# Places for round two's split weights taken after their words have landed, the order written with dearer table changes, and one subtraction moved to GpSimd

## Chip, cores and metric

One core of a Trainium2 chip runs the whole program. The metric is the device time of one execution in microseconds (us); lower is better. Engines: PE is TensorE, ACT is ScalarE, DVE is VectorE, POOL is GpSimd, SP is SyncE, which here issues DMAs only.

## Reference

Attention that keeps the 32 largest scores of each row, then two MLPs, all in fp32. Cut to what matters:

```python
# q, k, v: (2, 8, 576, 64)
scores = q @ k.T / sqrt(64)
kth    = 32nd largest score of each row
attn   = softmax(where(scores >= kth, scores, -1e9))
x = (attn @ v) as 1152 tokens x 512
h = x @ w_in;  x = (h * tanh(softplus(h))) @ w_out      # 512 -> 2048 -> 512, Mish
h = x @ w2_in; out = (relu(h) ** 2) @ w2_out            # 512 -> 2048 -> 512
```

The MLP weights come as float64 words and have to be made fp32 on the chip.

## The kernel before

The 1152 tokens go in four **rounds** of 256, 320, 320 and 256 tokens. A round is the attention of its tokens (four pairs of heads, each of 4 or 5 *tiles* of 128 rows by 576 scores; 72 tiles in all) and then its two MLPs: in-phase, out-phase, in-phase, out-phase, each over 8 of the 32 weight pieces of 512 KB. Attention of later rounds stands beside the MLPs of earlier ones. (The code counts rounds from 0; "round two" of the change is `r == 1`, here always called round 1.)

A tile: scores on PE (L466, tile `ps`), copied by ACT to `s`; the 32 largest found on DVE by four MAX8 and three MATCH_REPLACE8 (L480, L483, L484); two small POOL operations make `nm` (L495, L496); ACT makes the mask with Prelu and then Exp (both write `e`, L498 to L500); PE transposes `e`, ACT copies the result to `pt`, and PE multiplies by v (L563).

Weights: `convert` reads the float64 words of a piece (1024 KB), makes fp32 with two ACT operations (`cu` with Prelu, `raw` or `stage`) and one on DVE (L693), and writes them to DRAM as `kept` (512 KB). Round 0 multiplies with the fp32 words `w` themselves. Round 1 splits each piece into hi and lo parts (tile `wt`, three places): `fetch` loads `w` from `kept` (three places, tag `cf`), ACT copies hi (L744), POOL subtracts lo in four parts (L262), the matmuls of L781 use both, and `keep` writes both to DRAM (`both`, 1024 KB). Rounds 2 and 3 load hi and lo from `both`. From round 1 on the activations are split too: `xh`, `xl` and `gh`, `gl`; `gl` is a subtraction of 128x320 or 128x256 (`sub`, L255), on the engine that the letter of `GL` names for the round: "v" is DVE, "g" POOL.

ACT holds one table of functions at a time. Mish is in another table than Exp; the program holds an ACT_TABLE_LOAD wherever the next operation needs the other one, and one stands ahead of a Prelu that follows Mish too.

**What sets the order.** All engines run their instructions in the order in which they are written, and `Order` (L40 to L153) writes them: it plays the program with an assumed duration for every operation, and at each moment an engine takes the ready operation with the lowest rank. A generator yields `(engine, duration, rank, function[, table])`, a semaphore for a place, an event, or a number (a delay). An operation that names a table other than the current one has 4.0 added to its rank. Tile semaphores make the real waits; the played times decide the order alone.

```python
yield act(0.78, 8, e, s, AF.Prelu, bias=nm[:, 0:1], scale=UP, alpha=2.0 ** 120)   # names no table
yield act(0.85, 8, e, e, AF.Exp, "exp", ...)
yield act(1.07, 12, both[:, 0], w)                       # hi of round 1, rank 12
yield from wide(6, ALU.subtract, both[:, 1], w, ...)     # lo, four parts on POOL
```

Of the kernel before, what the change touches and what calls it, by code (L numbers as in the profile page):

```python
# [9 lines left out]
F32 = mybir.dt.float32  # L10
# [11 lines left out]
BUFS = {"s": 4, "e": 2, "r": 3, "w": 2, "kt": 2, "vt": 3, "qt": 2, "kT": 4, "cu": 4, "cf": 3, "wt": 3, "h": 3, "x1": 2, "pt": 1}  # L22
CONV_EVERY = 6.0
EARLY = 11
GL = "gvggg"
PARTS = 4


class Sem:
# [13 lines left out]
class Order:  # L43
# [69 lines left out]
    def issue(self, e):  # L113
        if self.free[e] > self.now or not self.ready[e]:
            return

        def rank(entry):
            x = entry[3]
            return ((x[2]() if callable(x[2]) else x[2]) + (4.0 if len(x) > 4 and x[4] != self.table else 0.0), entry[1])

        entry = min(self.ready[e], key=rank)
        self.ready[e].remove(entry)
        _, _, gen, x = entry
        value = self.written(x[3])
        t = x[1]
        if len(x) > 4 and x[4] != self.table:
            self.table = x[4]
            t += self.SWITCH
        self.free[e] = self.now + t
        self.last[gen] = e  # L130
        self.at(self.free[e], 0, lambda: self.step(gen, value))
        self.at(self.free[e], 1, lambda: self.issue(e))
# [32 lines left out]
def topk_attention_two_mlps(  # L165
# [50 lines left out]
    def give(*names):  # L216
        for t in names:
            sim.give(sems[t])
# [225 lines left out]
    def tile_of(p, j, a, rank, unit, pair):  # L444
# [50 lines left out]
            nc.gpsimd.tensor_scalar(out=nm[:, 0:1], in0=thr, scalar1=-UP, scalar2=None, op0=ALU.mult)  # L495
            nc.gpsimd.tensor_scalar(out=nm[:, 1:2], in0=thr, scalar1=mx[:, 0, 0:1], scalar2=scale, op0=ALU.subtract, op1=ALU.mult)  # L496

        yield ("POOL", 0.4, 1, biases)  # L498

        yield act(0.78, 8, e, s, AF.Prelu, bias=nm[:, 0:1], scale=UP, alpha=2.0 ** 120)  # L500
        give("s")
        yield act(0.85, 8, e, e, AF.Exp, "exp", bias=nm[:, 1:2], scale=scale / UP, accum_out=acc[:, a:a + 1])
        sim.set(unit[1][a])
# [27 lines left out]
    def unit_end(j, unit, pair):  # L531

        acc, _, done = unit[:3]
        yield sems["r"]
        r_ = new([P, 2, D], F32, "r")
        z = acc if j < 2 else acc[:, 0:1]
        yield ("POOL", 0.2, 1, lambda: nc.gpsimd.tensor_scalar(out=z, in0=z, scalar1=1e-9, scalar2=None, op0=ALU.add))
        yield ("DVE", 0.16, 3, lambda: nc.vector.reciprocal(z, z))
        if j < 2:
            sums = acc[:, 0:2].rearrange("p (a o) -> p a o", o=1).to_broadcast([P, 2, D])  # L540
            yield ("POOL", 0.4, 1, lambda: nc.gpsimd.tensor_tensor(out=r_, in0=sums, in1=one2, op=ALU.mult))
        else:
            yield act(0.3, 10, r_, same, scale=z)
        pair["r"][j] = r_.rearrange("p a d -> p (a d)")
        sim.set(unit[5])

    def pair_end(p, units, pair):
# [44 lines left out]

        yield act(evict_time(n), 9, inv[:, 0:n], pp[:, 0:n])
        give("ps_t")
        yield ("DVE", 0.6, 4, scaled)
        give("ps_x")
        x1_left[r] -= 1
# [71 lines left out]
    def convert(i):  # L669

        src, a, m = pieces[i]
        n = NW
        kind, at = raw_places.pop(0)
        if kind == "stage":
            both = stage[:, at * 2 * n:(at + 1) * 2 * n]
        else:
            both = new([P, 2 * n], F32R, "wt", "raw")
        raw = both.bitcast(I32).rearrange("p (m t) -> p m t", t=2)  # L680
        yield from sim.dma(lambda: nc.sync.dma_start(out=raw.rearrange("p (a m) t -> p a (m t)", a=a), in_=src), 1024, 20)
        yield sems["cu"]
        w = new([P, n], F32, "cu")
        lo, hi = raw[:, :, 0], raw[:, :, 1]
        R = 20 + 0.01 * i

        yield act(1.16, R, w, hi.bitcast(F32), AF.Prelu, scale=2.0 ** -112, alpha=-2.0 ** 32)

        yield act(1.16, R, lo, lo.bitcast(U32), bias=-0.499, scale=LOW3)
        wi = w.bitcast(I32)
        yield ("DVE", 1.65, lambda: 15 if x1_done[0].done or i < EARLY else 25, lambda: nc.vector.scalar_tensor_tensor(out=wi, in0=wi, scalar=3, in1=lo, op0=ALU.logical_shift_left, op1=ALU.bitwise_or))  # L693
        raw_places.append((kind, at))
        sim.give(raw_sem)
        kept[i] = dr.tile([P, n], F32, tag=f"k{i}", name=f"kept{i}")
        yield from sim.dma(lambda: nc.sync.dma_start(out=kept[i], in_=w), 512, 15)
        give("cu")
        sim.set(kept_done[i])
        if i == NP - 1:  # L700

            for d in kept_done:
                yield d
            for _ in range(BUFS["wt"]):
                sim.give(wt_sem)
            sim.set(stage_free)
# [6 lines left out]
            yield CONV_EVERY  # L713

    got = [Ev() for _ in range(NR * NP)]
    ready = {}

    def fetches():
        for i in range(NR * NP):
            r, j = divmod(i, NP)  # L720
            yield kept_done[j]
            yield (sems["cf"] if r == 0 else wt_sem)
            if r == 1:
                yield sems["cf"]
            if r > 1:
                yield both_done[j]
            sim.spawn(fetch(i, r, j))
            yield 0.3

    def fetch(i, r, j):  # L730

        if r < 2:
            w = new([P, NW], F32, "cf", "w")
            yield from sim.dma(lambda: nc.sync.dma_start(out=w, in_=kept[j]), 512, 12)
            ready[i] = [w]
        if r:
            both = new([P, 2, NW], F32R, "wt", "wt")
            ready[i] = [both[:, 0], both[:, 1]]
            if r == 1:
                yield act(1.07, 12, both[:, 0], w)  # L740
                yield from wide(6, ALU.subtract, both[:, 1], w, both[:, 0].bitcast(F32))
                give("cf")
                sim.spawn(keep(j, both, i))
# [265 lines left out]
```

## Time and profile before

| | us |
|---|---|
| median of 3 runs (lowest, highest) | 778.89 (775.28, 780.21) |
| the profiled execution | 773.01 |
| its span, first to last instruction | 771.2 |
| PE busy in the span | 649.1 |
| ACT, DVE, POOL busy | 513.1, 470.1, 249.2 |
| mean granted clock of PE | 0.931 of full speed |

Between the profiled execution and its span lie 1.8 us, taken as fixed. The span has five stretches by what the MLPs do: attention of round 0 alone (to 139 us), Mish of round 0 (to 197), the rest of round 0 (to 331), round 1 (to 551), rounds 2 and 3 (to the end). Round 1 divides at 415, 457 and 512 us into in, out, in and out-phase. A busy PE is counted from modelled ends of pipelined matmuls.

### The profile page before, as it was taken

The numbers are of one execution on the slowest core, as the hardware profiler recorded it, in microseconds if no ns is written. First come the engines' busy times: TensorE is split into PE (matmuls) and PEld (weight loads), VectorE is DVE, ScalarE is ACT, GpSimd is POOL, SyncE is SP. The second block draws the span as 40 slices with busy tenths as digits, with TensorE's granted clock in tenths as the row PEclk, the third lists the DMA queues.
The fourth block names the chain that finished last, engine by engine and source line by source line (L and its number), as shares of the span: only waits on it lengthen the run. The fifth ranks groups of instructions, "written<-read, shape, count | busy, mean of one in ns | idle before, by whom it ended". The sixth has DMA issues, their size and how long they took to land.

```text
span 771.2 us, 11656 instructions
## 1 busy us (share of the span) xinstructions
PE 649.1 (84%) x4056; PEld 569.3 (74%) x4056; DVE 470.1 (61%) x889; ACT 513.1 (67%) x917; POOL 249.2 (32%) x453
## 2 busy tenths in 40 slices
PE   5463565878997979976878998798999999999997
PEld 2342344666876767865777898687899999999997
DVE  3797999787887895998999999995100000100000
ACT  4797865699887976689999779875351272251540
POOL 2233122111221120445535667556341041040330
PEclk9975665999999989998889999899999999999999
DMA  7999920765799976675765688369988888899995
GB/s 199 285 338 329 348 58 18 264 247 164 260 306 364 311 251 199 192 229 167 255 192 207 229 293 301 141 250 338 340 309 295 289 311 292 299 338 366 343 358 196
DMA packets 95290, 201.83 MB, mean 262 GB/s; under 512 B 36352, under 2 KB 61440, under 8 KB 82944
## 3 DMA queue, kind: packets, MB, share of 16 engines
q1 hardware_dynamic: 94144, 200.83, 76.0%
q8 instruction: 32, 0.52, 0.3%
q10 hardware_dynamic: 1088, 0.26, 0.2%
q14 instruction: 26, 0.21, 0.1%
HBM read 146.01 MB, written 52.69 MB: 258 GB/s over the span
## 4 chain that ended last, share of the span: by engine, by line
PE 41%; DMA 22%; ACT 14%; DVE 11%; POOL 5%; SPq 4%; issue 2%; ACTq 0%; POOLq 0%; DVEq 0%
PE pm L781 33%; DMA w<-kept 8%; DMA wt<-both 5%; DVE w L483 4%; POOL wt L262 4%; DVE mx L484 4%; ACT e L249 3%; ACT L249 3%; PE ps L466 3%; SPq L311 2%; PE px L563 2%; ACT wt L249 2%; DMA kt<-in_k 1%; PE pt L509 1%; DMA raw<-in_moe_w_in 1%
## 5 line engine op out<-in xcount | busy, mean ns | idle before, releaser
L781 PE MATMUL pm<-xh,wt 128*128 128x320 f32 (+1 forms) x768 | 170.1, 308 | 2.9 <-DMA wt<-both 1.7
L484 DVE MAX8 mx<-w 128x8 f32<-128x576 f32 x216 | 164.4, 761 | 7.4
L781 PE MATMUL pm<-gh,wt 128*128 128x320 f32 (+1 forms) x768 | 166.0, 302 | 3.3 <-DMA wt<-both 1.2
L781 PEld LDWEIGHTS pm<-xh,wt 128*128 128x128 f32 x768 | 130.4, 194 | 4.3 <-ACT h L249 3.1
L781 PEld LDWEIGHTS pm<-gh,wt 128*128 128x128 f32 x768 | 126.7, 188 | 4.5 <-DMA wt<-both 2.2
L781 PE MATMUL pm<-xl,wt 128*128 128x320 f32 (+1 forms) x384 | 117.5, 306 | 0.2
L781 PE MATMUL pm<-gl,wt 128*128 128x320 f32 (+1 forms) x384 | 115.1, 300 | 0.0
L483 DVE MATCH_REPLACE8 w<-mx,w 128x576 f32<-128x576 f32 x144 | 106.9, 742 | 0.0
L262 POOL TENSOR_TENSOR wt<-w,wt 128x256 fp32r<-128x256 f32 x128 | 91.6, 742 | 35.9 <-ACT wt L249 30.2
L255 POOL TENSOR_TENSOR gl<-h,gh 128x320 fp32r<-128x320 f32 (+1 forms) x64 | 51.6, 806 | 147.7 <-ACT gh L249 111.3
L509 PE MATMUL pt<-ident,e 128*128 128x128 f32 x288 | 50.7, 305 | 43.0 <-ACT e L249 23.6
L509 PEld LDWEIGHTS pt<-ident,e 128*128 128x128 f32 x288 | 37.5, 154 | 53.2 <-ACT e L249 27.4
L249 ACT ACTIVATE h<-pm 128x320 f32<-128x320 f32 (+1 forms) x112 | 45.2, 413 | 45.8 <-PE pm L781 41.8
L781 PEld LDWEIGHTS pm<-xl,wt 128*128 128x128 f32 x384 | 74.4, 194 | 0.6 <-DVE xl L255 0.6
L781 PEld LDWEIGHTS pm<-gl,wt 128*128 128x128 f32 x384 | 72.3, 188 | 0.1
L962 DVE COPY ot<-pm 128x256 f32<-128x256 f32 x16 | 6.7, 421 | 105.1 <-PE pm L954 52.8
L249 ACT ACTIVATE pt<-pt 128x640 f32<-128x640 f32 x72 | 50.4, 700 | 28.3 <-PE pt L511 27.9
L255 DVE TENSOR_TENSOR xl<-pm,xh 128x320 fp32r<-128x320 f32 (+1 forms) x12 | 5.6, 463 | 101.0 <-ACT xh L249 101.0
L495 POOL TENSOR_SCALAR nm<-mx 128x1 f32<-128x1 f32 x72 | 25.1, 349 | 127.9 <-DVE mx L484 127.6
L781 PE MATMUL pm<-gh,w 128*128 128x256 f32 x256 | 62.2, 393 | 4.2 <-DMA w<-kept 4.2
L249 ACT ACTIVATE e<-s,nm 128x576 f32<-128x576 f32 x72 | 55.6, 772 | 14.5 <-POOL nm L495 14.0
L249 ACT ACTIVATE e<-e,nm 128x576 f32<-128x576 f32 x72 | 55.8, 776 | 6.4 <-POOL nm L496 0.5
(94 smaller groups left out, 1171.8 us busy)
## 6 DMA issues: line engine op xcount, KB each, us to landing
wt<-both SPq DMA_DIRECT2D x64, 1024.0 KB, 5.2
w<-kept SPq DMA_DIRECT2D x64, 512.0 KB, 5.9
both<-wt SPq DMA_DIRECT2D x32, 1024.0 KB, 4.9
kept<-cu SPq DMA_DIRECT2D x32, 512.0 KB, 7.0
raw<-in_moe_w_in SPq DMA_DIRECT2D x9, 1024.0 KB, 8.9
raw<-in_moe_w_out SPq DMA_DIRECT2D x9, 1024.0 KB, 8.3
stage<-in_moe_w_in SPq DMA_DIRECT2D x7, 1024.0 KB, 6.5
stage<-in_moe_w_out SPq DMA_DIRECT2D x7, 1024.0 KB, 9.4
```

Of the source, the lines that this page charges most:

```text
L249: op = ("ACT", t, rank, lambda: nc.scalar.activation(out, in_, func, **kw))
L255: return ({"g": "POOL", "v": "DVE"}[e], t, rank, lambda: eng.tensor_tensor(out=out, in0=in0, in1=in1, op=ALU.subtract))
L262: yield ("POOL", 0.05 + 0.0024 * n, rank, lambda: nc.gpsimd.tensor_tensor(out=out[:, z], in0=in0[:, z], in1=in1[:, z], op=op))
L311: f = lambda o=o, x=x, e=eng if i >= 3 else nc.sync: e.dma_start(out=o, in_=x)
L466: nc.tensor.matmul(sp[:, i, 0:HK], q_, k_[:, i * HK:(i + 1) * HK], start=l == 0, stop=l == len(steps) - 1)
L483: nc.vector.match_replace(out=w, in_to_replace=mx[:, i - 1, :], in_values=s if i == 1 else w, imm_value=LOWEST)
L484: nc.vector.max(out=mx[:, i, :], in_=w)
L495: nc.gpsimd.tensor_scalar(out=nm[:, 0:1], in0=thr, scalar1=-UP, scalar2=None, op0=ALU.mult)
L509: nc.tensor.transpose(pp[:, c * P:(c + 1) * P], e[:, c * P:(c + 1) * P], ident)
L563: nc.tensor.matmul(xo[a * D:(a + 1) * D, 0:n], vt[z, a, c, :], pt[z, a, c, 0:n], start=c == 0, stop=c == NK)
L781: nc.tensor.matmul(o, w[a], x[b], start=first and i == 0, stop=last and i == len(terms) - 1)
L962: yield ("DVE", 0.15 + 0.14 * nt, 4, lambda: nc.vector.tensor_copy(ot[:, i:i + nt, :], pp[:, i * P:(i + nt) * P].rearrange("p (j c) -> p j ...
```

## The change

Seven edits, all of them in what is played:

- `fetches` and `fetch`: round 1 takes a place for the words `w` first, loads, and takes the place for hi and lo only when the words have landed; round 2 starts to fetch when all of round 1's places are taken (`all_placed`).
- The hi copy of round 1 has rank 7 in place of 12: ahead of the attention's copies (8 to 10).
- Both Prelu operations name the table "exp".
- A table change adds 7.0 to a rank (`STAY`) in place of 4.0.
- `GL` is "ggggg": `gl` of round 1 goes from DVE to POOL.
- The played durations of three small POOL operations are longer (0.4 to 0.7, 0.2 to 0.35, 0.4 to 0.45).
- Delays of 3.0 and 1.5 us (`SLACK`) are played ahead of two small DVE operations, the reciprocal (L538) and the scaling of the attention's output (L591).

```diff
-GL = "gvggg"
+GL = "ggggg"
+SLACK = 3.0
+STAY = 7.0
...
-            return ((x[2]() if callable(x[2]) else x[2]) + (4.0 if len(x) > 4 and x[4] != self.table else 0.0), entry[1])
+            return ((x[2]() if callable(x[2]) else x[2]) + (STAY if len(x) > 4 and x[4] != self.table else 0.0), entry[1])
...
-        yield ("POOL", 0.4, 1, biases)
-
-        yield act(0.78, 8, e, s, AF.Prelu, bias=nm[:, 0:1], scale=UP, alpha=2.0 ** 120)
+        yield ("POOL", 0.7, 1, biases)
+
+        yield act(0.8, 8, e, s, AF.Prelu, "exp", bias=nm[:, 0:1], scale=UP, alpha=2.0 ** 120)
...
+        yield SLACK
         yield ("DVE", 0.16, 3, lambda: nc.vector.reciprocal(z, z))
...
+        yield SLACK / 2
         yield ("DVE", 0.6, 4, scaled)
...
-        yield act(1.16, R, w, hi.bitcast(F32), AF.Prelu, scale=2.0 ** -112, alpha=-2.0 ** 32)
+        yield act(1.16, R, w, hi.bitcast(F32), AF.Prelu, "exp", scale=2.0 ** -112, alpha=-2.0 ** 32)
...
-            yield (sems["cf"] if r == 0 else wt_sem)
-            if r == 1:
-                yield sems["cf"]
+            if (r, j) == (2, 0):
+                yield all_placed
+            yield (sems["cf"] if r < 2 else wt_sem)
...
+            if r == 1:
+                yield wt_sem
+                if j == NP - 1:
+                    sim.set(all_placed)
             both = new([P, 2, NW], F32R, "wt", "wt")
             ready[i] = [both[:, 0], both[:, 1]]
             if r == 1:
-                yield act(1.07, 12, both[:, 0], w)
+                yield act(1.07, 7, both[:, 0], w)
```

Because the whole order is found anew, instructions stand elsewhere on every engine. Three places follow.

ACT in round 0's Mish phase; `gh<-pm` is Mish, `e` the attention's Prelu and Exp. Before:

```order
L249 ACT_TABLE_LOAD
L249 ACTIVATE gh<-pm 128x256
L249 ACTIVATE s<-ps 128x576
L249 ACT_TABLE_LOAD
L249 ACTIVATE e,acc<-e,nm 128x576
L249 ACT_TABLE_LOAD
L249 ACTIVATE gh<-pm 128x256
L249 ACT_TABLE_LOAD
L249 ACTIVATE e<-s,nm 128x576
L249 ACT_TABLE_LOAD
L249 ACTIVATE gh<-pm 128x256
```

The same place now:

```order
L251 ACT_TABLE_LOAD
L251 ACTIVATE e<-s,nm 128x576
L251 ACTIVATE e,acc<-e,nm 128x576
L251 ACTIVATE s<-ps 128x576
L251 ACT_TABLE_LOAD
L251 ACTIVATE gh<-pm 128x256 x3
L251 ACTIVATE pt<-pt 128x10x64
L251 ACT_TABLE_LOAD
L251 ACTIVATE e<-s,nm 128x576
L251 ACTIVATE e,acc<-e,nm 128x576
L251 ACTIVATE s<-ps 128x576
```

Two or three Mish operations now stand together, and Prelu and Exp of a tile stand side by side. In this phase the program holds 12 table loads where it held 18, in round 1's Mish phase 8 where it held 14.

SP's queue early in round 1, which takes its DMAs in this order (`w<-kept` the words of a piece, `both<-wt` its hi and lo on their way to DRAM; the digit behind `kept` and `both` is the piece). Before:

```order
L734 DMA w_2846<-kept3_367 128x1024
L319 DMA vt_2771<-in_v 128x256 x2
L319 DMA vt_2771<-in_v 64x2x64
L734 DMA w_2923<-kept4_431 128x1024
L752 DMA both3_2963<-wt_2913 128x2048
L734 DMA w_2978<-kept5_474 128x1024
```

Now:

```order
L739 DMA w_2676<-kept3_367 128x1024
L761 DMA both0_2674<-wt_2613 128x2048
L739 DMA w_2716<-kept4_431 128x1024
L761 DMA both1_2715<-wt_2666 128x2048
L977 DMA out_x<-ot_2703 256x1x128
L739 DMA w_2779<-kept5_474 128x1024
```

The words of piece 3 now stand ahead of the write of piece 0; before, they stood behind the writes of pieces 0 to 2.

The subtraction `gl` in round 1. DVE before, among the search for the largest (`mx`, `w`):

```order
L483 MATCH_REPLACE w<-mx,w 128x576
L484 MAX mx<-w 128x8
L255 TENSOR_TENSOR gl<-h,gh 128x320 x3
L480 MAX mx<-s 128x8
L483 MATCH_REPLACE w<-mx,s 128x576
```

POOL now, among the parts of lo (`wt<-w,wt`):

```order
L264 TENSOR_TENSOR wt<-w,wt 128x256 x2
L257 TENSOR_TENSOR gl<-h,gh 128x320 x2
L264 TENSOR_TENSOR wt<-w,wt 128x256 x2
L497 TENSOR_SCALAR nm<-mx 128x1
L498 TENSOR_SCALAR nm<-mx 128x1
```

All 32 `gl` of round 1 have left DVE. How many of the attention's tiles (counted by Exp on ACT) stand beside each phase of round 1, from the split of its input to the last copy of its output: in the in, out, in, out-phase 12, 7, 8 and 4 before, and 6, 9, 10 and 6 now; 41 tiles stand ahead of it in both, and none behind it.

## Rows read from the trace of the kernel before

**Rows 1.** Busy time of all five stretches. Columns: stretch, length, PE, PEld, DVE, ACT, POOL, PEclk, DMA share, GB/s
```profile
139.00:197.00 58.00, 46.88 (x242) 37.94 (x241) 45.24 (x83) 53.47 (x78) 7.19 (x23) 0.97 0.68 232
197.00:331.00 134.00, 121.45 (x648) 99.30 (x647) 110.80 (x200) 104.69 (x188) 33.38 (x71) 0.97 0.85 276
331.00:551.00 220.00, 192.35 (x1286) 171.74 (x1285) 190.34 (x376) 176.88 (x316) 122.98 (x221) 0.95 0.68 240
551.00:772.00 221.00, 210.69 (x1563) 207.19 (x1561) 11.47 (x30) 79.94 (x186) 51.61 (x64) 1.00 0.85 309
0.00:139.00 139.00, 77.73 (x326) 53.15 (x327) 112.28 (x203) 98.07 (x152) 34.05 (x75) 0.74 0.71 218
```
**Rows 2.** The same view, round 1 by its four phases
```profile
331.00:415.00 84.00, 66.92 (x418) 56.75 (x416) 77.24 (x152) 76.96 (x131) 40.34 (x76) 0.90 0.57 190
415.00:457.00 42.00, 41.83 (x295) 39.32 (x295) 40.16 (x82) 33.41 (x59) 26.74 (x49) 1.00 0.77 269
457.00:512.00 55.00, 47.30 (x326) 42.34 (x327) 52.98 (x103) 47.83 (x99) 33.38 (x60) 0.94 0.73 262
512.00:551.00 39.00, 36.30 (x252) 33.32 (x252) 19.96 (x42) 18.68 (x31) 22.52 (x38) 1.00 0.78 283
```
**Rows 3.** Waits of PE, 139 to 197 us: engine line waited for, total us, times, longest
```profile
PE ps L466 <- ACT s L249: 9.1, 5, 2.8
```
**Rows 4.** Groups by line, 139 to 197 us: count, busy us, mean ns, idle before
```profile
L249 ACT ACT_TABLE_LOAD x18 | 23.1, 1283 | 0.7 <-DMA kept<-cu 0.4
```
**Rows 5.** Timeline of ACT in Mish of round 0: start us, us, instruction
```profile
148.18 1.16 ACT L249 ACTIVATE cu<-stage 128x1024 f32<-128x1024 f32 x1
149.24 0.76 ACT L249 ACTIVATE e<-s,nm 128x576 f32<-128x576 f32 x1
150.02 1.28 ACT L249 ACT_TABLE_LOAD   x1
151.31 0.38 ACT L249 ACTIVATE gh<-pm 128x256 f32<-128x256 f32 x1
```
**Rows 6.** Waits of PE, 331 to 415 us
```profile
PE ps L466 <- ACT s L249: 8.1, 5, 3.1
```
**Rows 7.** Groups by line, 331 to 551 us
```profile
L249 ACT ACTIVATE wt<-w 128x1024 fp32r<-128x1024 f32 x30 | 31.4, 1052 | 5.9 <-DMA w<-kept 4.7 <-issue 1.1
L249 ACT ACTIVATE e<-e,nm 128x576 f32<-128x576 f32 x31 | 24.1, 777 | 2.6
L249 ACT ACTIVATE e<-s,nm 128x576 f32<-128x576 f32 x31 | 23.9, 772 | 10.5 <-POOL nm L495 10.4
L249 ACT ACTIVATE pt<-pt 128x640 f32<-128x640 f32 x34 | 23.8, 700 | 7.1 <-PE pt L511 6.9
L255 DVE TENSOR_TENSOR gl<-h,gh 128x320 fp32r<-128x320 f32 x32 | 19.9, 659 | 1.7 <-ACT gh L249 1.7
L249 ACT ACTIVATE s<-ps 128x576 f32<-128x576 f32 x27 | 17.1, 634 | 0.0
```
**Rows 8.** Tile gl, whole span, on DVE: min/median/max ns, first and last start
```profile
L255 DVE TENSOR_TENSOR gl<-h,gh x32: 471/482/1759, 348.4 to 518.0; 128x320 fp32r<-128x320 f32 x32
```
**Rows 9.** L255 on POOL, round 2: min/median/max ns
```profile
L255 POOL TENSOR_TENSOR gl<-h,gh x32: 870/878/883, 555.9 to 640.9; 128x320 fp32r<-128x320 f32 x32
```
**Rows 10.** Tile mx, round 1: length, DVE, POOL, PEclk, DMA share, GB/s
```profile
331.00:551.00 220.00, 164.46 (x304) 20.34 (x62) 0.95 0.68 240
```
**Rows 11.** Tile wt, round 1: length, PE, PEld, ACT, POOL, PEclk, DMA
```profile
331.00:551.00 220.00, 127.17 (x766) 117.25 (x767) 31.37 (x30) 86.14 (x121) 0.95 0.68 240
```
**Rows 12.** Tile gl, first and third phase of round 1: PE, PEld, DVE, POOL
```profile
331.00:415.00 84.00, 0.00 (x0) 0.00 (x0) 8.36 (x13) 0.00 (x0) 0.90 0.57 190
...
457.00:512.00 55.00, 0.00 (x0) 0.00 (x0) 8.46 (x15) 0.00 (x0) 0.94 0.73 262
```
**Rows 13.** DMA issues: count, KB each, median us from issue to landing
```profile
w<-kept SPq DMA_DIRECT2D x64, 512.0 KB, 5.9
both<-wt SPq DMA_DIRECT2D x32, 1024.0 KB, 4.9
```
**Rows 14.** Busy time around the start of round 2
```profile
550.00:555.00 5.00, 4.30 (x28) 3.73 (x27) 1.70 (x4) 3.23 (x7) 0.00 (x0) 1.00 0.99 401
555.00:560.00 5.00, 4.15 (x29) 3.92 (x28) 0.61 (x2) 2.18 (x5) 1.75 (x2) 1.00 0.89 320
```

More of the change, by code (lines that the diff above doesn't have):

```diff
@@ L536, in unit_end @@
         z = acc if j < 2 else acc[:, 0:1]
-        yield ("POOL", 0.2, 1, lambda: nc.gpsimd.tensor_scalar(out=z, in0=z, scalar1=1e-9, scalar2=None, op0=ALU.add))
+        yield ("POOL", 0.35, 1, lambda: nc.gpsimd.tensor_scalar(out=z, in0=z, scalar1=1e-9, scalar2=None, op0=ALU.add))
+        yield SLACK
         yield ("DVE", 0.16, 3, lambda: nc.vector.reciprocal(z, z))
@@ L540, in unit_end @@
             sums = acc[:, 0:2].rearrange("p (a o) -> p a o", o=1).to_broadcast([P, 2, D])
-            yield ("POOL", 0.4, 1, lambda: nc.gpsimd.tensor_tensor(out=r_, in0=sums, in1=one2, op=ALU.mult))
+            yield ("POOL", 0.45, 1, lambda: nc.gpsimd.tensor_tensor(out=r_, in0=sums, in1=one2, op=ALU.mult))
         else:
@@ L715, in topk_attention_two_mlps @@
     got = [Ev() for _ in range(NR * NP)]
+    all_placed = Ev()
     ready = {}
```

## Prediction

> **What bounds the kernel now.** I read the busy times by stretch first, then the waits of PE, then the groups of the stretches that the change touches. [rows 1] divide the span. In rounds 2 and 3 (551 to 772) PE is busy 210.69 of 221 us and DVE hardly works: PE alone sets that stretch, and nothing of the change reaches into it. From 0 to 139 DVE is the fullest engine (112.28) beside ACT (98.07), on the attention of round 0. Between them, 139 to 551, PE is idle 11.1, 12.6 and 27.7 us; only those 51 us, and what PE loses at the lower of its two clock levels, can be won there.
>
> The three middle stretches have different limits. In Mish of round 0 (139 to 197) ACT is busy 53.47 of 58, and PE's largest wait is for ACT to empty the scores, 9.1 us [rows 3]: ACT sets the pace, and 23.1 us of its time are 18 table loads [rows 4]. From 197 to 331 the DMA share is 0.85 and PE is busy 121 of 134: close to full on both. In round 1, [rows 2] show the fullest engine changing: in the first phase DVE and ACT (77.24 and 76.96 of 84, with PE again waiting for ACT, [rows 6], at a mean granted clock of 0.90, so part of it at 1.2 GHz rather than 2.4), in the second PE (41.83 of 42), in the third DVE (52.98 of 55), in the fourth PE (36.30 of 39).
>
> **The change part by part.**
>
> *Front, to 139 us.* Up to the first Mish the order holds the same work: 18 tiles started on DVE and 11 conversions before the last output of round 0's attention, as before. I take 0.
>
> *Table loads in round 0.* The program has 12 where it had 18. One load is 1283 ns [rows 4], so 6 x 1.283 = 7.7 us of the engine that sets the pace. It can't be more than this by much, since ACT stood idle only 0.7 us ahead of all 18 loads. It can be less: two or three Mish now stand together, so PE's three places for results fill while ACT is at the tiles. What lies beside has room: DVE 45.2 and PE 46.9 of 58, less 7.7 is 50.3 us of stretch, which still holds both. I take 7, between 2 and 7.7; it carries through the next stretch only if the conversions start earlier too, which they do, as their number at the end of Mish is 17 in both orders.
>
> The Trainium skill, page "ScalarE: Activation LUTs", section "What ACT_TABLE_LOAD costs", gives a change of table about 2.66 us, since a drain of 1.38 goes with the load. [rows 5] speak against it: a load begins at 150.02, where the operation before it ends (149.24 + 0.76), and the next begins at 151.31, 0.01 us after the load's end. By that page the six loads would give 16 us, by the trace 7.7; I go by the trace.
>
> *gl from DVE to POOL.* 32 subtractions leave DVE: 19.9 us at a mean of 659 ns [rows 7] (median 482, the longest 1759 [rows 8]). On POOL the same shape takes 878 ns [rows 9], so POOL gets 32 x 0.878 = 28.1 us on top of 122.98 in 220 us. That is 151, still the least loaded engine over the whole round, but not in each phase (below).
>
> The page "GPSIMD Engine Reference" of the Trainium skill, section "Engine selection", would leave such an operation on VectorE: with two inputs GpSimd is about twice as slow. Against the mean of 659 the trace gives 878 / 659 = 1.33. By the page's factor POOL would get 32 x 1.32 = 42 us, 7 more in each of the two in-phases, which would take about 4 us off what round 1 gains below; by the trace nothing more.
>
> *Words ahead of the places.* The transfer of 5.9 us [rows 13] leaves the round trip of a place; the write of hi and lo (4.9) stays in it. Taken directly this is worth little: hi waited for data only 5.9 us in total over 30 copies [rows 7], and PE's waits in the round are for ACT. Its effect is through the order: because the weights are played as ready earlier, the first in-phase now holds 6 tiles of attention, not 12, and the other phases 9, 10 and 6 instead of 7, 8 and 4. On SP the words of piece i+3 now stand ahead of the write of piece i; both can go once lo of piece i is done, so I charge nothing for that.
>
> *hi at rank 7.* Same copies, 1.05 us each [rows 7], earlier in ACT's queue. Behind an early hi stand the copies of scores and of `pt`, for which PE waits. Cost: from 0 to a full landing of a write, 4.9 us, for each of 29 copies (the first three find free places). The nearest row is the 5.9 / 30 = 0.2 us that one waited before; I take 0, since the place is now played as free first, and keep the rest for a rival.
>
> *Round 1 by phases.* Cost of one tile. ACT: 0.777 + 0.772 + 0.634 + 0.700 = 2.9 us [rows 7]. DVE: 164.46 / 31 = 5.3 [rows 10]. POOL: 20.34 / 31 = 0.7 [rows 10]. PE: what is busy beyond the matmuls with `wt`, (192.35 - 127.17) / 31 = 2.1 [rows 1, 11]. Then, from [rows 2] and the shift of tiles:
> First in-phase, 6 tiles less, 6 loads less (7.7), gl off DVE (8.36 [rows 12]) and 16 of them on POOL (14.0): ACT 76.96 - 17.4 - 7.7 = 51.9; DVE 77.24 - 31.8 - 8.4 = 37.0; PE 66.92 - 12.6 = 54.3; POOL 40.34 - 4.2 + 14.0 = 50.1. Fullest: PE, 54.
> First out-phase, 2 tiles more: DVE 40.16 + 10.6 - 1.9 = 48.9; PE 46.0. Fullest 49.
> Second in-phase, 2 more: DVE 52.98 + 10.6 - 8.5 = 55.1; ACT 53.6; PE 51.5; POOL 33.38 + 1.4 + 14.0 = 48.8. Fullest 55.
> Second out-phase, 2 more: PE 36.30 + 4.2 = 40.5; DVE about 29. Fullest 41.
> The sum is 199. The same sum before is 77.2 + 41.8 + 53.0 + 36.3 = 208.3, and the round took 220, 1.056 times that. With the same loss it takes 199 x 1.056 = 210: 10 us gained. If it loses nothing, 21; at the first phase's own loss before, 84 / 77.2 = 1.09, it takes 217 and gains 3. I take 10. Note what this says of the moved subtractions: DVE is freed of 20 us, but starves in the first phase, and most of what it won it needs later.
>
> *Start of round 2.* Its first load now stands behind the last place of round 1 and the last write. PE loses 0.70 and 0.85 us in the 10 us there [rows 14]; I charge 1 us more, between 0 and a landing of 5.
>
> *SLACK and the longer played POOL times* act on the order only and are in the counts above.
>
> Sum: 7 + 10 - 1 = 16 us. Against the profiled execution 773.0 - 16 = 757.0. The runs shown have a median of 778.89, 1.0076 times the profiled one, so 757.0 x 1.0076 = 762.8, told as 763.
>
> **Rivals** (times on the scale of the median).
> *POOL takes DVE's place.* In both in-phases POOL comes to 50 and 49 us, within 4 to 6 us of the fullest engine, and `nm`, lo and gl share one queue: a gl that waits for its `gh` holds up the `nm` for which the next Exp waits. For it: ACT already waited 10.4 us for `nm` in this round [rows 7]. Against: `nm` stands first by rank, and lo is cut in four. Round 1 then gains nothing, and only round 0's 7 are left: 772.
> *hi blocks ACT (the slower side).* hi now stands ahead of the attention's copies; if its place is not free when ACT comes to it, ACT stands, and PE behind it. The price of one is between 0.2 and 4.9 us; it cancels the gain of 16 at 16 / 29 = 0.55 us a copy, and decides for slower by over 1% at (16 + 8) / 29 = 0.83. The geometric middle of the ends is 0.99, so 29 us: 763 + 29 = 792. For it: in [rows 6] PE's waits are for ACT already. Against: 0.2 us before, with a transfer in the chain that has now left it.
> *The phases run into one another.* Nothing forbids attention to flow over a phase's edge, and PE at full clock would need less in the first phase. Round 1 then takes the bare 199 us and gains 21: 773.0 - 7.7 - 21 = 744.3, on the median's scale 750.
> *Table loads cost more than their row.* If each of the 12 that go freed its drain too, 1.38 us more, ACT gets 8 more in round 0 (in round 1 PE is then the fuller engine): 755. It is the rule of the page on ScalarE named above. Only the gap of 0.01 us in [rows 5] bears on it, and against it.
>
> **How the numbers follow.** Forecast 0.47, POOL 0.20, hi 0.12, phases run together 0.17, dearer loads 0.04. The forecast's own bounds are the sums of its ends: gains of 7.7 + 21 = 28.7 and of 2 + 3 - 5 = 0. The low end of the range takes in the third rival, 748; the high end covers the second to where it begins to decide and leaves the rest of the hi rival out: 782. A measurement of this kernel can tell about 1% from no change, here 771 and 787. Below 771 lie the two better rivals (0.21) and about 0.42 of the forecast, with a little of POOL's case, which sits at the edge: 0.66. Above 787 lies most of the hi rival and the tail of POOL's: 0.12. The rest, 0.22, is no change.
>
> **What would show it.** Right: Mish of round 0 takes about 51 us with 12 loads, ACT still near full; round 1 about 210 us, its first phase below 60 with POOL busy about 50 in it, its second and third longer than before; rounds 2 and 3 at 220. Wrong: hi copies with long waits for the write `both` or for PE; `nm` idle rows grown on ACT; DVE idle in the first phase and still at the search when round 1's MLPs are through; or PE's clock lower where its waits are longer.

## The result, and the profile after

The changed kernel takes 743.04 us in the median (737.7 to 745.65, 4 runs) against 778.0 of the kernel before in the same comparison: a ratio of 0.9543, interval 0.9478 to 0.9609. 35 us are gone where 16 were forecast, and 743 lies outside the stated 748 to 782. Run again later (e9 below) it gave 743.28, a ratio of 0.9634 (0.9584 to 0.9685). The profiled execution is 741.41, its span 739.6.

Busy time of the changed kernel between four of its own marks (first output of round 0's out-phase at 193 us, last one of its second MLP at 318, last one of round 1 at 523); columns as in [rows 1]:

```profile
141.00:193.00 52.00, 49.29 (x263) 40.52 (x262) 49.41 (x90) 48.65 (x79) 10.83 (x25) 1.00 0.72 256
193.00:318.00 125.00, 117.36 (x623) 96.32 (x621) 106.19 (x190) 101.10 (x179) 31.45 (x63) 0.97 0.86 285
318.00:523.00 205.00, 189.96 (x1291) 169.11 (x1291) 174.34 (x346) 169.41 (x314) 147.52 (x258) 0.98 0.78 272
523.00:740.00 217.00, 209.63 (x1559) 206.93 (x1559) 11.39 (x30) 79.75 (x186) 51.78 (x64) 1.00 0.85 307
```

PE's work in round 1 is what it was, 189.96 us against 192.35 [rows 1]; its idle time fell from 27.7 to 15.0 us and its mean clock rose from 0.95 to 0.98. The same stretches of both kernels, by the same marks (the first mark is the last output of round 0's attention; all from the timelines of DVE and ACT):

| mark, us | before | changed | length before | length changed | difference |
|---|---|---|---|---|---|
| round 0's attention done | 137.4 | 140.5 | 137.4 | 140.5 | +3.1 |
| first output of out-phase, round 0 | 200.5 | 192.7 | 63.1 | 52.2 | -10.9 |
| last output of round 0's MLPs | 327.9 | 318.1 | 127.4 | 125.4 | -2.0 |
| last output of round 1's MLPs | 551.6 | 522.8 | 223.7 | 204.7 | -19.0 |
| end of span | 771.2 | 739.6 | 219.6 | 216.8 | -2.8 |

A second profile of the changed kernel puts the marks at 139.4, 191.6, 316.5, 524.5 and 740.3: a stretch repeats within 4 us, so the first, third and last differences say little. Between its mark at 327.9 and the first split of round 1's input (330.95 us, where [rows 1] and the prediction cut at 331) the kernel before still starts one tile's Exp; in the changed kernel the split follows at once, at 318.33. Cut there, with 31 tiles behind the cut in both, round 1 is 220.7 us before and 204.5 now, 16.2 less, and the rest of round 0 is 4.8 less.

Round 1 by its four phases:

```profile
318.00:375.00 57.00, 51.25 (x326) 45.61 (x328) 45.19 (x88) 51.33 (x94) 49.03 (x78) 0.94 0.79 274
375.00:421.00 46.00, 43.97 (x315) 40.01 (x312) 43.62 (x89) 38.00 (x66) 30.35 (x58) 1.00 0.91 323
421.00:483.00 62.00, 56.05 (x369) 49.48 (x369) 59.81 (x117) 55.23 (x111) 50.63 (x87) 0.97 0.83 280
483.00:523.00 40.00, 38.70 (x283) 34.02 (x283) 25.71 (x55) 24.85 (x47) 17.50 (x37) 1.00 0.54 196
```

Against [rows 2] the first phase went from 84 to 57 us, the two middle ones grew by 4 and 7, the last by 1. In the first phase ACT is busy 51.33 (forecast 51.9), PE 51.25 (54.3), POOL 49.03 (50.1); but DVE is busy 45.19 where 37.0 was forecast. PE's largest wait is the one of [rows 3] and [rows 6], smaller; here from 139 to 197 us and from 318 to 375:

```profile
PE ps L468 <- ACT s L251: 1.7, 2, 1.0
...
PE ps L468 <- ACT s L251: 3.6, 3, 1.5
```

9.1 us became 1.7, and 8.1 became 3.6. Groups of round 1, as in [rows 7]:

```profile
L251 ACT ACTIVATE wt<-w 128x1024 fp32r<-128x1024 f32 x30 | 31.7, 1056 | 8.0 <-PE pm L790 6.3 <-POOL gl L257 0.9 <-DMA w<-kept 0.4
L251 ACT ACTIVATE e<-s,nm 128x576 f32<-128x576 f32 x31 | 23.8, 770 | 0.7 <-PE pt L513 0.3 <-POOL nm L497 0.2
L257 POOL TENSOR_TENSOR gl<-h,gh 128x320 fp32r<-128x320 f32 x32 | 27.6, 875 | 4.1 <-ACT gh L251 4.0
L482 DVE MAX8 mx<-s 128x8 f32<-128x576 f32 x30 | 22.4, 746 | 10.5 <-ACT s L251 10.3
```

A wait has taken another's place: hi (first row) waited 4.7 us for its words before, and now 0.4 for them but 6.3 for PE to free the place. Over 30 copies that is 0.2 us each, as before; the second rival needed 0.83. The last row shows DVE starving in the first phase, as forecast (10.3 us, in one wait of 9.3 and a short one).

One wait is all but gone, and the prediction had no term for it. Ahead of the small reciprocal (L538, now L541) DVE stood idle until POOL had finished the sum that it inverts; the whole span, before and now:

```profile
DVE acc L538 <- POOL acc L537: 30.5, 17, 6.4
...
DVE acc L541 <- POOL acc L539: 0.7, 2, 0.5
```

The two played delays and the longer played POOL times (`SLACK`) put that reciprocal later in DVE's order. e7 below takes them out again.

### The profile page after: what moved, and what is told of

Read it like the earlier page. It is cut to its first block, busy times and chain, and to the rows that moved or that the text cites. A ratio compares the mean times of both kernels' runs of the same rounds, so it can differ in the third digit from the quotient of the medians.

```text
span 739.6 us, 11640 instructions
## 1 busy us (share of the span) xinstructions
PE 642.7 (87%) x4056; PEld 565.8 (76%) x4056; DVE 454.2 (61%) x857; ACT 496.1 (67%) x905; POOL 274.8 (37%) x485
## 4 chain that ended last, share of the span: by engine, by line
PE 50%; DVE 16%; DMA 15%; ACT 8%; POOL 4%; issue 3%; SPq 3%; ACTq 0%; POOLq 0%
PE pm L790 40%; DVE w L485 7%; DVE mx L486 6%; DMA wt<-both 5%; DMA w<-kept 3%; PE ps L468 3%; PE px L566 3%; ACT e L251 2%; POOL wt L264 2%; DMA kept<-cu 2%; PE pt L511 2%; DMA kt<-in_k 2%; DVE mx L482 2%; SPq L313 1%; DMA raw<-in_moe_w_out 1%
## 5 line engine op out<-in xcount | busy, mean ns | idle before, releaser
L790 PE MATMUL pm<-xh,wt 128*128 128x320 f32 (+1 forms) x768 | 168.2, 305 | 4.9 <-ACT h L251 2.6
L790 PE MATMUL pm<-gh,wt 128*128 128x320 f32 (+1 forms) x768 | 169.4, 304 | 0.8 <-DMA wt<-both 0.5
L257 POOL TENSOR_TENSOR gl<-h,gh 128x320 fp32r<-128x320 f32 (+1 forms) x96 | 79.4, 831 | 150.1 <-ACT gh L251 113.1
L790 PEld LDWEIGHTS pm<-xh,wt 128*128 128x128 f32 x768 | 128.1, 190 | 7.6 <-ACT h L251 4.3
L251 ACT ACTIVATE h<-pm 128x320 f32<-128x320 f32 (+1 forms) x112 | 45.9, 412 | 47.0 <-PE pm L790 43.8
L497 POOL TENSOR_SCALAR nm<-mx 128x1 f32<-128x1 f32 x72 | 23.4, 325 | 123.5 <-DVE mx L486 102.9
L482 DVE MAX8 mx<-s 128x8 f32<-128x576 f32 x72 | 53.7, 746 | 20.4 <-ACT s L251 20.2
L790 PE MATMUL pm<-gh,w 128*128 128x256 f32 x256 | 59.5, 382 | 0.3 <-DMA w<-kept 0.3
```

The costliest lines, as they stand in the source:

```text
L251: op = ("ACT", t, rank, lambda: nc.scalar.activation(out, in_, func, **kw))
L257: return ({"g": "POOL", "v": "DVE"}[e], t, rank, lambda: eng.tensor_tensor(out=out, in0=in0, in1=in1, op=ALU.subtract))
L482: nc.vector.max(out=mx[:, 0, :], in_=s)
L790: nc.tensor.matmul(o, w[a], x[b], start=first and i == 0, stop=last and i == len(terms) - 1)
```

## The experiments

18 kernels ran. Each ratio is to the kernel before, timed beside it; all the draws and parts are in one table at the end of this section. "Order kept" means that every engine's instructions stand as in the kernel named, but for the edit. A *draw* is one order that the play finds: where a played number is changed, the whole order is found anew.

**What a table load costs, order kept (e1, e2).** Behind three Mish operations a one-element Exp is put, so that each time two loads come in:

```diff
-                yield act(evict_time(n), 9, g[0][:, i, 0:n], o, AF.Mish, "mish")
+                def first():
+                    nc.scalar.activation(g[0][:, i, 0:n], o, AF.Mish)
+                    if i in (0, 3, 8):
+                        nc.scalar.activation(tiny, one, AF.Exp)
+
+                yield ("ACT", evict_time(n), 9, first, "mish")
```

> The changed kernel with the order on every engine kept, and six more table loads in Mish of round 0 (18 in place of 12): behind three Mish operations a one-element Exp is put, whose result is used nowhere. It prices a load where ACT sets the pace. Theory A (the prediction's step): a load costs its own 1.28 us and no more, so 7.7 us and some 0.6 for the three small Exp, 743 to 751. Theory B (a load costs a drain too, or holds PE's places for results so long that PE loses the time twice): 2.6 us or more a load, 759 or above. Theory C (ACT does not set the pace in the new order): under 3 us, 746.

Measured 749.67 (748.24 to 751.05), ratio 0.9682 (0.9654 to 0.971). From the first load to the last Mish it is 45.9 us, against 37.5 and 37.4 in two profiles of the changed kernel: 8.4 for six loads and three small Exp. The timeline of ACT in e1 shows what such a pair is made of:

```profile
146.97 0.38 ACT L893 ACTIVATE gh<-pm 128x256 f32<-128x256 f32 x1
147.36 1.28 ACT L895 ACT_TABLE_LOAD   x1
148.65 0.20 ACT L895 ACTIVATE tiny<-one 128x1 f32<-128x1 f32 x1
148.87 1.28 ACT L893 ACT_TABLE_LOAD   x1
150.17 0.38 ACT L893 ACTIVATE gh<-pm 128x256 f32<-128x256 f32 x1
```

From 147.36 to 150.17 are 2.81 us, two loads of 1.28 and the Exp of 0.20, with 0.05 between: there is no drain beside the load. 6 x 1.28 + 3 x 0.2 = 8.3, theory A to a tenth. The rival of the page "ScalarE: Activation LUTs" of the Trainium skill (section "What ACT_TABLE_LOAD costs", about 2.66 us a change) would have made it 16 and falls.

The same in round 1, where `i in (2, 5, 9)` and `r == 1`:

> The same in Mish of round 1: 14 loads in place of 8, the rest of the order kept. Theory A: ACT and PE are about equally full there (52 and 54 us by the prediction's sum), so most of the 7.7 us show: 748 to 751. Theory B: 16 us or more, 759. Theory C (the attention that was moved behind the first phase gives it slack, and a longer first phase is made good later): under 3 us, 746.

751.25 (748.99 to 752.02), ratio 0.9693 (0.9659 to 0.9726): 8 us, theory A at its upper edge. By the profile round 1 itself is 210.5 us long, 6 more than in one profile of the changed kernel and 2.5 more than in the other. So the 12 loads that the change removes from the two Mish phases are worth some 14 us in this order: 6.4 and 8.0 by the medians, against the 743.28 of e9, with the small Exp operations in them. No run has all 12 put back at once.

**Which engine does gl, order kept (e3, e15).** e3 gives the 32 subtractions to DVE in the changed order, e15 gives them to POOL in the old one:

```diff
-            yield sub(GL[r], n, 5, g[1][:, i, 0:n], h[:, 0:n], g[0][:, i, 0:n].bitcast(F32))
+            yield sub(GL[r], n, 5, g[1][:, i, 0:n], h[:, 0:n], g[0][:, i, 0:n].bitcast(F32), nc.vector if r == 1 else None)   # e15: nc.gpsimd
```

> The changed kernel with its order kept, but the 32 subtractions gl of round 1 given to DVE at the same places of the order. Theory A (DVE is the fullest engine in the second and third phase, so its 20 us matter there only): 8 to 12 us slower, about 753. Theory B (the move to POOL is neutral, the gain is all in the order): within 3 us of 743. Theory C (DVE sets all of round 1): the whole 16 to 20 us of DVE, about 761.

748.03 (745.7 to 750.13), ratio 0.966 (0.9626 to 0.9694): some 5 us slower than the changed kernel, between A and B, and its interval overlaps that of e9. Round 1 is 211.5 us long, and the difference sits in the third phase (67 us against 62), where DVE is the fullest engine, with 64.58 us.

> The kernel before with its order kept, but the 32 subtractions gl of round 1 given to POOL at the places where DVE had them. Theory A (DVE is one of two fullest engines in the first and third phase of the old order): 4 to 10 us faster, 764 to 770 where the kernel before has 774. Theory B (ACT and PE set the length, DVE's time is covered): within 3 us. Theory C (POOL's queue holds up nm and lo): slower.

779.92 (774.11 to 785.03) where the kernel before has 775.51, ratio 1.005 (1.0014 to 1.0087): theory C, though only by 4 us, and not through `nm` (ACT waited 9.7 us for it, 10.4 before). Round 1 is 229.8 us long, not 223.7. DVE is busy 17.7 us less in it (175.61 against 193.27), but stands ahead of the reciprocal instead; round 1 of the kernel before, then of e15:

```profile
DVE acc L538 <- POOL acc L537: 4.6, 5, 2.0
...
DVE acc L538 <- POOL acc L537: 24.5, 12, 4.0
```

What POOL's queue holds up is the sum that DVE waits for, and that eats the 20 us won. In the old order the move pays nothing; in the changed one that wait is gone.

**One part undone, order found anew (e4 to e7, e17).**

```diff
-STAY = 7.0                 # e4: and both Prelu without "exp"
+STAY = 4.0
...
-            yield (sems["cf"] if r < 2 else wt_sem)        # e5: and the wait for wt_sem behind the load goes
+            yield (sems["cf"] if r == 0 else wt_sem)
+            if r == 1:
+                yield sems["cf"]
...
-                yield act(1.07, 7, both[:, 0], w)          # e6
+                yield act(1.07, 12, both[:, 0], w)
...
-SLACK = 3.0                # e7: and 0.7, 0.35, 0.45 of POOL are 0.4, 0.2, 0.4 again
+SLACK = 0.0
...
-GL = "ggggg"               # e17
+GL = "gvggg"
```

> The changed kernel with one part undone and the order found anew: a table change adds 4.0 to a rank again and the two Prelu name no table. The program then has 38 loads, not 22 (18 and 16 in the two Mish phases). Theory A at 1.28 us a load: 16 loads are 20.5 us of ACT, of which those in round 0 show fully and those in round 1 mostly: 758 to 763. Theory B at 2.6 us a load: about 780, the whole gain gone. Theory C (the gain comes from the words ahead of the places, the loads are covered): under 750.

780.27 (779.1 to 782.43), ratio 1.0064 (1.002 to 1.0107): the whole gain is gone. That is 37 us for 16 loads, 20.5 us of ACT; nearer to B's number, but e1 has shown that B's reason is wrong. What makes up the rest is not shown: the order was found anew.

> The changed kernel with one part undone and the order found anew: round 1 takes the place for hi and lo before the words are fetched, as before; hi keeps rank 7. By the order the first phase of round 1 then holds 9 tiles of attention, not 6, and 10 table loads, not 8. Theory A (the transfer of 5.9 us was covered; the part acts through the order alone): 3 tiles more in the first phase, ACT 8.7 us and loads 2.6 us fuller there and less full later, so 4 to 8 us slower, about 749. Theory B (the round trip of the three places limits round 1): 32 pieces / 3 places x 5.9 us = 63 us of round trips, of which a third shows: 760 or above. Theory C (neutral): within 3 us.

758.07 (754.22 to 760.11), ratio 0.9765 (0.9693 to 0.9837): 15 us above the changed kernel, between A and B.

> The changed kernel with hi of round 1 at rank 12 again, order found anew: the first phase of round 1 holds 9 tiles, not 6. Theory A (rank 7 is what keeps lo and the matmuls supplied): 4 to 8 us slower, about 749. Theory B (an early hi blocks ACT at times, so rank 12 is better): 2 to 5 us faster, about 739. Theory C: within 3 us of 743.

758.5 (757.27 to 760.98), ratio 0.9777 (0.9722 to 0.9833): 15 us, beyond all three theories.

> The changed kernel without the two played delays and with the old played times of the three small POOL operations, order found anew. Mish of round 0 then begins one tile of attention earlier in the order, as before the change. Theory A (they act on the order only and are worth little): within 4 us of 743. Theory B (they keep DVE and POOL from standing at operations whose input comes late in truth): 8 us or more slower, 751 or above, with more idle time of DVE ahead of the reciprocal and the scaling.

766.86 (765.06 to 771.6), ratio 0.9891 (0.9829 to 0.9953): 24 us. Most of its loss is not in round 1 (210.8 us) but in the rest of round 0, which ends at 341.7 and not at 318.1 and holds two tiles of attention more. The sign that theory B names is there: DVE stands ahead of the reciprocal as in the kernel before,

```profile
DVE acc L541 <- POOL acc L539: 24.3, 14, 4.3
```

and in all 20 profiles here this wait is 0.5 to 7.7 us with the delays in the play and 19 to 47 us without them. What the wait costs in time is not shown: 16.8 of the 24.3 us lie in round 1, and e13 below, with 19.1, is as fast as e16, with 6.4.

> The changed kernel with gl of round 1 on DVE again and the order found anew for it: 12 and 8 loads as in the changed kernel, phases of round 1 with 6, 6, 12 and 6 tiles. Theory A (the part is worth some 5 us, as with the order kept, beside the draw of an order): 743 to 765, in the range of the other draws. Theory B (DVE's 20 us set round 1): 765 or above.

751.46 (749.18 to 753.15), ratio 0.9684 (0.9618 to 0.9749). Round 1 is 205.4 us long in it, as short as in the changed kernel, with DVE busy 190.63 of 206: DVE's 20 us do not set round 1. One tile of attention is left over behind round 1 in this order, and rounds 2 and 3 take 224.1 us, not 216.8.

**How much is the draw of an order (e8, e10, e11, e16 for the changed kernel; e12 and e18 for the one before).** No part is undone; only the played time of a table load is off:

```diff
-    SWITCH = 1.3
+    SWITCH = 1.4        # e8, e12; e10 1.2, e11 1.25, e16 and e18 1.35
```

> A control: the changed kernel with one played number off by a little (a table load is played as 1.4 us, not 1.3), so that an order is found anew with no part of the change undone. It shows how much of the differences between kernels is the luck of an order. Theory A: within 4 us of 743, so that differences of 8 us are parts of the change. Theory B (luck of the order is as large as the parts): 8 us or more away.

758.54 (755.1 to 763.43), ratio 0.9779 (0.9711 to 0.9846): theory B. This is the experiment that changes the reading of all those before it: an order that lacks nothing of the change is 15 us slower, as much as an order with the words or the rank undone. So e5 and e6 cannot tell a part from a draw, and with the next draw (767) neither can e7.

> A second draw of the control: the changed kernel with a table load played as 1.2 us. Its order has the same 12 and 8 loads in the two Mish phases; in round 1 the phases hold 8, 10, 11 and 1 tiles, near the first control's 7, 10, 11 and 1 (the changed kernel: 6, 9, 10 and 6). Theory A (the spread of tiles over the phases of round 1 sets its length): near the first control, 755 to 762. Theory B (the first control was an unlucky draw): 743 to 748.

767.07 (764.01 to 769.67), ratio 0.9922 (0.9891 to 0.9952), slower than either theory had it.

> A third draw: a table load played as 1.25 us; phases of round 1 hold 8, 6, 10 and 6 tiles, the last two as in the changed kernel. Theory A (six tiles left for the last out-phase, where PE and DVE have room, are what makes round 1 short): 743 to 750. Theory B (luck of many small waits): anywhere in 743 to 762, not told by the tiles.

752.91 (752.31 to 758.1), ratio 0.9758 (0.9711 to 0.9805): above A's band, inside B's; the six tiles of the last phase alone do not make round 1 short.

> A further draw of the changed kernel's order: a table load played as 1.35 us; phases of round 1 hold 8, 10, 11 and 1 tiles, as in the two draws that came to 758 and 767. Theory A (one tile left for the last out-phase, 11 in the second in-phase): 755 to 767. Theory B (the tiles do not tell): 743 to 755.

758.84 (755.25 to 763.08), ratio 0.9817 (0.9756 to 0.9878): A.

> The changed kernel unaltered, beside the three other kernels of this call on the same chip: 743, a ratio of 0.95 to 0.96 to the kernel before. It anchors the differences of the other experiments, which were each compared with the kernel before alone.

743.28 (741.91 to 747.18), ratio 0.9634 (0.9584 to 0.9685): as it was. The changed kernel's own order is a good one, and reproducibly so: the four other draws lie 10 to 24 us above it, at 759.3 in the mean.

> The same control on the kernel before: a table load played as 1.4 us, no part of the change in it. Its order has 16 and 18 loads in the Mish phases, against 18 (and 14) in the kernel before, and the phases of round 1 hold 7, 11, 9 and 4 tiles. Theory A (the parts of the change are worth about 20 us and the rest of the 35 is the draw of two orders): 768 to 785. Theory B (the kernel before had an unlucky order): 755 to 768.

766.65 (762.47 to 769.56), ratio 0.9899 (0.9865 to 0.9932): under A's band and inside B's. The kernel before, too, has a draw better than its own, by 7 us in the medians.

> A draw of the kernel before with a table load played as 1.35 us; its order happens to hold 46 loads, not 34 (18 and 24 in the two Mish phases, 42 against 32). Theory A (1.28 us a load where ACT is among the fullest engines): 12 loads more are 15 us, 782 to 795 where the kernel before has 775. Theory B (in the old order of round 1 ACT has room and loads are covered): 770 to 780.

803.52 (801.73 to 804.47), ratio 1.0363 (1.0305 to 1.042): 28 us for 12 loads more, above A. The expectation counted the loads of the Mish phases by two rules; by one rule, from the first load to the last Mish, round 0 has 17 in the kernel before and 19 here. What is sure is the total, 46 against 34: two more in Mish of round 0 and ten more in round 1. The loads are not the whole of it. The rest of round 0, which holds no load in either kernel, takes 142.4 us, not 127.4: 15 of the 28. Three tiles more lie ahead of its end, and PE waits longer for the words there; before, then e18:

```profile
PE pm L781 <- DMA w<-kept: 8.7, 5, 4.2
...
PE pm L781 <- DMA w<-kept: 14.4, 6, 3.7
```

So e18 is a bad draw beside its loads, and does not price them.

**One part alone in the kernel before, order found anew (e13, e14).** The same edits as above, put into the old kernel.

> The kernel before with the table part alone: a change adds 7.0 to a rank and both Prelu name the table. 24 loads in all against 34 (12 and 10 in the two Mish phases). Theory A (1.28 us a load, as the added loads cost): 10 x 1.28 = 13 us, less a little, 760 to 766 where the kernel before has 774. Theory B (draws of an order decide): anywhere from 755 to 780, and not told by the loads; then Mish of round 0 still has to be about 38 us long, as it is in every order with 12 loads, and round 1 gives the rest away.

759.83 (755.86 to 766.4) against 775.51, ratio 0.9822 (0.9761 to 0.9882): 16 us, at the edge of A's band and inside B's. A draw of the kernel before without the part (e12) is 7 us better too, so this run alone cannot price the part.

> The kernel before with the words ahead of the places and hi at rank 7, tables as before: 36 loads in all, phases of round 1 with 8, 6, 10 and 6 tiles. Theory A (weights played as ready earlier shorten the first phase of round 1 and the whole round by some 8 us): 764 to 770 where the kernel before has 774. Theory B (worth nothing without the cheaper table changes, since ACT is then full in the first phase with 16 loads): 772 to 780.

776.51 (773.2 to 781.79), ratio 1.0014 (0.9982 to 1.0045): B, nothing, although the first in-phase has 8 tiles rather than 12. It is a draw as well, so it does not show that the part is worth nothing in every order.

All of it in one table; "Mish" is from the first table load to the last Mish of round 0, "round 1" from the last output of round 0's MLPs to that of round 1's, both from the timeline of ACT in one profile; tiles in the first phase by the order.

| kernel | median | loads | Mish | round 1 | tiles |
|---|---|---|---|---|---|
| before | 773.5 to 778.0 | 34 | 51.6 | 223.7 | 12 |
| e14 words alone | 776.5 | 36 | 52.4 | 225.4 | 8 |
| e15 gl on POOL, order kept | 779.9 | 34 | 53.0 | 229.8 | 12 |
| e12 before, other draw | 766.7 | 36 | 49.4 | 226.3 | 7 |
| e18 before, other draw | 803.5 | 46 | 55.0 | 230.0 | 11 |
| e13 tables alone | 759.8 | 24 | 43.4 | 215.1 | 10 |
| changed | 743.0 | 22 | 37.5 | 204.7 | 6 |
| e9 changed again | 743.3 | 22 | 37.4 | 208.0 | 6 |
| e3 gl on DVE, order kept | 748.0 | 22 | 37.4 | 211.5 | 6 |
| e1 six loads more | 749.7 | 28 | 45.9 | 204.7 | 6 |
| e2 six loads more | 751.3 | 28 | 39.0 | 210.5 | 6 |
| e17 gl undone | 751.5 | 22 | 37.5 | 205.4 | 6 |
| e11 other draw | 752.9 | 22 | 41.2 | 212.2 | 8 |
| e5 words undone | 758.1 | 24 | 39.0 | 216.3 | 9 |
| e6 hi rank 12 | 758.5 | 22 | 37.5 | 220.1 | 9 |
| e8 other draw | 758.5 | 22 | 38.2 | 219.1 | 7 |
| e16 other draw | 758.8 | 22 | 37.7 | 214.6 | 8 |
| e7 slack undone | 766.9 | 20 | 43.1 | 210.8 | 6 |
| e10 other draw | 767.1 | 22 | 38.2 | 224.4 | 8 |
| e4 tables undone | 780.3 | 38 | 46.5 | 224.5 | 7 |

Two things are plain in it. Mish of round 0 is 37 to 43 us with the dearer table changes and 46 to 55 without them or with loads put in there, in every draw. And round 1 is 205 to 212 us wherever the first phase holds 6 tiles and Mish there has few loads, 212 to 224 with 7 to 10 tiles, and about 224 or more with the loads of the old rules. The second is seen across orders that differ in more than that, so it is a pattern and not a test; e7's round is short with two tiles fewer to do in it, since they went ahead. A slow draw of the changed kernel, e10, in its first phase (324 to 397 us):

```profile
324.00:397.00 73.00, 59.79 (x364) 52.44 (x365) 64.56 (x127) 60.25 (x109) 47.49 (x81) 0.88 0.71 250
```

and PE's largest wait in that phase:

```profile
PE ps L468 <- ACT s L251: 13.4, 6, 5.4
```

The first phase takes 73 us, not 57, and the wait of PE for ACT to empty the scores is 13.4 us, not 3.6, with a granted clock of 0.88 in place of 0.94: with more tiles beside the phase, PE stands in its fixed order at scores that ACT has not emptied yet. That the tiles are the cause is a reading of these rows and not shown.

## Why the prediction was wrong, and where it was right

Right in direction, and wrong in size. Its sum for round 1 by phases was 54, 49, 55 and 41 at the bare fullest engine; the fullest engine came to 51.33 (ACT), 43.97 (PE), 59.81 (DVE) and 38.70 (PE). ACT, PE and POOL of the first phase came within about 3 us of the forecast; DVE had 8 us more there, 5 less in the second phase and 5 more in the third, so counting tiles by their Exp on ACT did not place DVE's search. That POOL would take 28 us without becoming the bound (27.6 came) and that hi would wait no longer than before held. That the fetch is worth nothing directly fits its 0.2 us a copy, but no run with the order kept tests it. On the profiles' own scale it forecast 757.0 and 741.4 came, 15.6 us less. By its terms, with round 1 cut at the split of its input as the prediction has it (0.8, 4.8, 6.2 and 3.8 us of the 15.6):

- *"Table loads in round 0 ... I take 7, between 2 and 7.7"*: -10.9 us measured to the first output of the out-phase. The size of a load was right (e1); beyond the six loads one tile of attention had moved ahead of Mish (18 Exp before the first Mish, not 17), where the front grew by 3.1, which the step "Front: I take 0" left out. The two together are -7.8, near the forecast.
- *Rest of round 0, not charged*: -4.8 (-5.3 in the second profile). Why is not shown.
- *"The sum is 199 ... With the same loss it takes 199 x 1.056 = 210 ... I take 10"*: this is the step that failed. The round came to 205 us, 16.2 less (12.9 in the second profile). The same loss did hold: 51.33 + 43.97 + 59.81 + 38.70 = 193.8, and 205 is 1.058 times that. What was mis-sized is the sum, 193.8 for 199: 3 and 5 us less in the first two phases, 5 more in the third, 2 less in the fourth. That the loss held is this order's luck: worked out in the same way, the four other draws of the same kernel (e8, e10, e11, e16) take 1.07 to 1.1 times a sum of 193 to 202, and their rounds are longer than the 210 forecast.
- *Start of round 2, 1 us charged*: rounds 2 and 3 took 2.8 us less; PE's waits for `wt` went from 2.9 to 1.0 us there. Why is not shown.
- *"SLACK and the longer played POOL times act on the order only"*: put at nothing without a row. DVE's wait ahead of the reciprocal went from 30.5 to 0.7 us. How much of the gain this is stays open.
- *The scale of 1.0076 from the profiled execution to the median* added 5.8 us, of which the changed kernel has 1.6 (741.41 against 743.04).

The second profile repeats the first three phases and has its fourth at a granted clock of 0.88, not 1.00, at 44 us for 40:

```profile
317.00:373.00 56.00, 51.60 (x327) 46.88 (x327) 44.43 (x84) 50.61 (x92) 48.41 (x77) 0.91 0.79 271
373.00:418.00 45.00, 43.95 (x315) 40.00 (x311) 43.48 (x88) 37.31 (x63) 29.67 (x57) 1.00 0.91 322
418.00:480.00 62.00, 54.94 (x369) 48.08 (x369) 59.19 (x116) 55.46 (x113) 51.24 (x88) 1.00 0.82 283
480.00:524.00 44.00, 42.69 (x282) 36.71 (x282) 26.26 (x56) 24.91 (x46) 17.44 (x37) 0.88 0.49 180
```

And the range. Its ends were sums of the terms' ends, for the one order at hand, and its gains ended at 28.7; 31.6 came on the profiles' scale. (Its high end, 782, is said to be where the hi rival begins to decide; by that rival's own prices this is 779 or 787.) That an order found anew moves the time by itself had no term, though the change was said to find every order anew. With e8, e10, e11 and e16 the changed kernel has draws from 743 to 767, about 12 us to either side of their middle; the kernel before has 767 (e12), 775 and, with 12 loads more, 804 (e18). The 16 us forecast are also what lies between the kernel before and the mean of the four other draws, 775 less 759, but that is luck and no confirmation: either kernel's draws spread further than this. What is shown is that the 12 loads cost 6.4 and 8.0 us put back into the good order (e1, e2), somewhat under half of the 30 to 35 us. That the rest is few tiles in round 1's first phase is what the table suggests; that it is the reciprocal's wait is what e7 suggests. Both stay open as causes.

Of the rivals, *POOL takes DVE's place* fell with 743 (ACT waited 0.2 us for `nm` in round 1, and 2.5 for `gl`); in the old order it came true by another wait (e15). *hi blocks ACT* fell with 0.2 us a copy. *The phases run into one another* had the nearest number, 750, but not the reason: the round came to 205 with its loss in place, on a smaller sum. *Loads cost more than their row* fell with e1. The rule of the page "GPSIMD Engine Reference" (Trainium skill, "Engine selection"), about twice as slow with two inputs, weighed 4 us: POOL took 875 ns where DVE took a mean of 659, 1.33 times, though against DVE's median of 482 [rows 8] it is 1.82, near the page's. With the order kept the move brought 5 us in the new order and cost 4 in the old.

## What to carry to other kernels

When a table of numbers orders a whole program anew, first measure what a new order is worth by itself: shift a number that ought not to matter and time two or three draws, of the old kernel and of the new. Only what exceeds their spread, here 24 us for the changed kernel and 37 for the one before, may be told as a part's own gain, and undoing a part tells little unless the order is kept. Tests that keep the order, with a load put in or one operation on another engine, separate causes to within a few us, where the draws do not; but they hold for that order, as the move of `gl` shows, worth 5 us in one and -4 in the other. And look at each engine's waits before and after, also for a part that was put at nothing.

## What the runs showed of the hardware

A table load cost its 1.28 us and 0.01 to 0.02 us around it, and in Mish of round 0, where ACT was busy 37.16 of 38.3 us, all of it came out in the length of the stretch (8.4 us for 6 loads and 3 small operations; 6.4 us in the median of the kernel). The transfers changed when the words went ahead:

```profile
w<-kept SPq DMA_DIRECT2D x64, 512.0 KB, 5.3
both<-wt SPq DMA_DIRECT2D x32, 1024.0 KB, 7.4
```

The writes of hi and lo take 7.4 us to land in the changed kernel, not 4.9 [rows 13], since the words go ahead of the places: the median is 6.4 to 7.6 us in every kernel with that part (e14 and e6 among them) and 4.8 to 4.9 in every one without it (e5, which lacks only that part, among them). The words of a later piece now stand ahead of a write in SP's queue. That both move at once is not enough of a reason, as 22 of the 32 writes met a load of words before as well, at the same 4.9 us. ACT did not wait longer for it: a place was waited for only 0.2 us a copy, and for PE.
